# Score products of an attention kernel: the second head issued first, the first head's held behind it, in every item

## Chip, cores and metric

One core of a Trainium2 chip runs the whole program. The metric is the device time of one execution in microseconds (us). The kernel before took 1007.86 us, the median of 3 runs (1007.46 to 1009.16). About 0.2% (2.0 us) is what a measurement of this kernel can tell from no change.

## What is computed

Attention with a threshold, then two feed-forward layers, all in float32. Cut to what matters:

```python
# q, k, v: 4 batches, 8 heads, 576 positions, 64 per head
scores = (1 / sqrt(64)) * q @ k.T
thresh = max(scores, axis=-1) - tau
scores = where(scores >= thresh, scores, -1e9)
attn = exp(scores - max(scores));  attn /= sum(attn) + 1e-9
x = (attn @ v)            # as 2304 tokens x 512
h = x @ w_in              # 512 x 1024
solu = h * softmax(h);  ln = layernorm(solu) * g_ln
x2 = ln @ w_out           # 1024 x 512
y = softplus(x2 @ w2_in) @ w2_out   # 512 x 2048, 2048 x 512
```

## The kernel before, in words

Two heads make a pair: head 0 lies in partitions 0 to 63 of the tiles `q` and `k`, head 1 in partitions 64 to 127. The attention is cut into 36 items (`items`), each one pair of heads with one or two tiles of 128 query rows and, in some, a tail of 64 rows. Items 0 to 7 (`n < 2 * NPAIR`) have one tile each; the later ones have two, and 16 of those carry a tail (items 8 to 11, 16 to 19 and 24 to 31).

For each tile `scores` (L167 to L190) makes the 128 x 576 scores of both heads, each head in two matmuls of 288 columns (`nh` 0 and 1). Each is a float32 product, and in the trace it is two instructions of TensorE, so that a tile of both heads is eight instructions of L177. Head 0 goes to the PSUM tile `s0`, head 1 to `s1`; each has one buffer. A tail takes `s0` for both heads. VectorE then takes the row maximum of each head (`nm`, L187), ScalarE the exponential (`E`, L188), which frees the PSUM tile, and VectorE masks and sums (L195, in `mask`, up to one tile later).

Behind an item's scores come, for the item before it, the reciprocal of its sums (`rinv`, L238 and L239; `rb`, L245), the transposes of its exponentials (L210, L219, L221, L231, L250, copied out by ScalarE at L212, L224, L252), and for the item before that the product with `v` (L276, in `av`), which VectorE scales into `xr` (L279).

`m1_units` runs beside it: as soon as a unit of 256 tokens has all its heads, TensorE makes h (L355, twelve matmuls into one bank `w`), ScalarE copies it (L357), VectorE takes its maximum (`m_nm`, L367) and so on; L390 transposes, L403 makes `x2`. `prep_w1` splits the first layer's weights into two parts on VectorE (L81, L82, L84, L88, L118) and ScalarE (L80, L87); it fills the first 120 us. The second layer follows from about 500 us on (L573, L612).

The order in which the instructions stand on each engine is not the order of this code: a scheduler of the tile framework places them, by what it expects each tile's readiness to be. Engines take their instructions in that order, and wait by semaphores.

The flag `apart` decides the order of the four matmuls of a tile: head 0's two and then head 1's for items 0 to 7, the heads in turn (head 0 first) for the others. Nothing keeps the scheduler from placing something else between them.

Of the kernel before, what the change touches and what calls it, by code (L numbers as in the profile page):

```python
# [20 lines left out]
NPAIR = H // 2  # L21
# [12 lines left out]
def tile_attention_solu_softplus(ctx: ExitStack, tc: tile.TileContext, q, k, v, tau, w_in, w_out, g_ln, w2_in, w2_out, out):  # L34
    nc = tc.nc
    PSUM = bass.MemoryType.PSUM
    pe, dve, act, pool, sp = nc.tensor, nc.vector, nc.scalar, nc.gpsimd, nc.sync
# [107 lines left out]
    def qcol(h, i):  # L145
        return P * i if h == 0 else (64 + P * i if i < 4 else 0)
# [6 lines left out]
    def begin(n):  # L153
        it = Item()
        it.n = n
        it.b, h, it.ts, it.tail = items[n]
        it.p = it.b * NPAIR + h
        it.h = h
        it.nt = len(it.ts)
        it.W = P * it.nt  # L160
        it.E = []
        it.e = {}
        it.sums = at.tile([P, 5], F32, tag="sums", name=f"sums{n}", bufs=3)
        it.rinv = at.tile([P, 5], F32, tag="rinv", name=f"rinv{n}", bufs=3)
        return it

    def scores(it, k_, apart):  # L167
        z = st[it.p]
        tail = k_ == it.nt
        i = 4 if tail else it.ts[k_]  # L170
        ps = [psS.tile([P, 2, 512], F32, tag=f"s{h}", name=f"s{it.n}_{k_}_{h}") for h in range(1 if tail else 2)]
        order = [(nh, h) for h in range(2) for nh in range(2)] if apart else [(nh, h) for nh in range(2) for h in range(2)]
        for nh, h in order:
            r, c, m = slice(64 * h, 64 * h + 64), qcol(h, i), 64 if tail else P
            kc = (64 if h == 1 and tail else 0) + 288 * nh
            o = ps[0][r, nh, 0:288] if tail else ps[h][:, nh, 0:288]
            pe.matmul(o, z["q"][r, c:c + m], z["k"][r, kc:kc + 288], start=True, stop=True)  # L177
        if tail:
            it.T = at.tile([P, 640], F32, tag="T", name=f"T{it.n}")
        else:  # L180
            it.E.append(at.tile([P, 1152], F32, tag="E", name=f"E{it.n}_{k_}", bufs=4))
        for h in range(len(ps)):
            s = 2 * k_ + h
            E = it.T[:, 0:576] if tail else it.E[k_][:, 576 * h:576 * h + 576]
            sv = ps[h][:, :, 0:288]
            nm = at.tile([P, 1], F32, tag="nm", name=f"nm{it.n}_{s}", bufs=4)
            dve.tensor_reduce(out=nm, in_=sv, axis=AX.XY, op=ALU.max, negate=True)  # L187
            act.activation(out=E.rearrange("p (a b) -> p a b", a=2), in_=sv, func=AF.Exp, bias=nm, scale=1.0)  # L188
            pend.append((E, it.sums[:, s:s + 1]))
        return len(ps)  # L190

    def mask(keep):
        while len(pend) > keep:
            E, acc = pend.pop(0)
            dve.scalar_tensor_tensor(out=E, in0=E, scalar=etau, in1=E, op0=ALU.is_ge, op1=ALU.mult, accum_out=acc)  # L195
# [99 lines left out]
    def attention():  # L295
        cur = prev = pp = None
        for n in range(NI + 2):
            pp, prev, cur = prev, cur, (begin(n) if n < NI else None)
            work = []
            if prev is not None:  # L300
                per = 4 // prev.nt
                work.append(lambda: rinv(prev))
                if not prev.tail:
                    work.append(lambda: xrest(prev))
                for c0 in range(0, 8, per):
                    work.append(lambda c0=c0: xgroup(prev, c0))
                if prev.tail:
                    work += [lambda: xrest(prev), lambda: xtail(prev)]
                work.append(lambda: rgroup(prev))
            nk = cur.nt + cur.tail if cur is not None else 0  # L310
            slots = max(2 * nk, 1)
            for s in range(slots):
                if s % 2 == 0:
                    keep = scores(cur, s // 2, n < 2 * NPAIR) if cur is not None else 0
                    mask(keep)
                if s == 0 and pp is not None:
                    av(pp)
                    if last_use[pp.p] == pp.n and pp.b + 1 < B:
                        load_v(pp.p + NPAIR)

                a = len(work) * max(s - 1, 0) // max(slots - 1, 1) if slots > 1 else 0
                e_ = len(work) * s // (slots - 1) if slots > 1 else len(work)
                if s or slots == 1:
                    for w in work[a:e_]:
                        w()
                if s == slots - 1 and cur is not None:
                    m = n + 1
                    if m < NI and items[m][0] > 0 and (m == 0 or items[m - NPAIR][0] != items[m][0]):
                        scale_q(items[m][0] * NPAIR + items[m][1])
                yield  # L330
            if cur is not None and last_use[cur.p] == cur.n and cur.b + 1 < B:
                load_qk(cur.p + NPAIR)
# [291 lines left out]
    for i in range(len(seq) + LA):  # L624
        if i < len(seq):
            bi, c = seq[i]
# [64 lines left out]
```

## Time and profile before

| | us |
|---|---|
| median of 3 runs | 1007.86 |
| the profiled execution | 1010.33 |
| its span, first to last instruction | 1008.5 |
| TensorE (PE) busy | 948.4 (94%) |
| weight loads (PEld) busy | 747.2 (74%) |
| VectorE (DVE) busy | 713.4 (71%) |
| ScalarE (ACT) busy | 568.9 (56%) |
| mean granted TensorE clock | 0.971 of full speed |

A busy matmul is not TensorE at its peak: matmuls are pipelined, so that one row's time holds the tail of its pipeline, and the time from one start to the next tells what a run of them takes. Rows with an x and a number are several instructions in a row; in brackets stands the idle time of the engine before them and what ended it.

### The profile page before, as it was taken

To read this page: it belongs to the slowest core of one execution; us is meant where nothing else is said; L and a number is where in the kernel's file an instruction comes from. 1 tells how busy PE (TensorE), PEld (TensorE's weight loads), DVE (VectorE), ACT (ScalarE), POOL (GpSimd) and SP (SyncE) were. 2 spreads that over 40 slices of the span, in tenths; PEclk is the share of its full clock that TensorE was granted. 3 is DMA by queue.
4 is the path that set the end of the run, shared out by engine and by line. 5 is a ranking of instruction groups with operands and counts; after the bars stand their busy time and mean duration, and the time that the engine had idled before them with its cause. 6 is when DMAs were issued, how large, how long until landed. Compare 5 with 4: busy or idle time off the path is not lost.

```text
span 1008.5 us, 14610 instructions
## 1 busy us (share of the span) xinstructions
PE 948.4 (94%) x5664; PEld 747.2 (74%) x5664; DVE 713.4 (71%) x1387; ACT 568.9 (56%) x1082; POOL 75.1 (7%) x47
## 2 busy tenths in 40 slices
PE   3898999999999999999997699898999999999997
PEld 2666567777677777876886588676888788888896
DVE  5898866766768577676589959976555755665565
ACT  4765666666657567566556546544444444444453
POOL 0000000000000000000033534311001000000000
PEclk8898899999999999999998799998999999999999
DMA  8412200112001220000054533302000100100010
GB/s 220 173 61 79 75 27 12 35 44 78 27 11 36 65 69 15 12 11 6 33 162 141 162 127 103 125 1 84 1 0 22 63 1 1 42 1 0 1 44 21
DMA packets 27125, 55.21 MB, mean 55 GB/s; under 512 B 3248, under 2 KB 12464, under 8 KB 27056
## 3 DMA queue, kind: packets, MB, share of 16 engines
q1 hardware_dynamic: 26896, 53.99, 17.1%
q8 instruction: 44, 0.72, 0.3%
q10 hardware_dynamic: 160, 0.30, 0.1%
q14 instruction: 25, 0.20, 0.1%
HBM read 44.83 MB, written 9.44 MB: 54 GB/s over the span
## 4 chain that ended last, share of the span: by engine, by line
PE 67%; DVE 18%; ACT 8%; issue 3%; DMA 2%; SPq 0%; DVEq 0%; ACTq 0%
PE y L612 12%; PE h L573 12%; PE s L177 10%; PE w L355 9%; PE w L403 8%; PE w L276 7%; PE w L210 5%; DVE u L82 2%; DVE w L584 2%; DVE t L585 2%; DVE w L591 2%; DMA raw<-in_w_in_dram 2%; DVE u L84 2%; DVE w L592 1%; DVE gl L594 1%
## 5 line engine op out<-in xcount | busy, mean ns | idle before, releaser
L177 PE MATMUL s<-k,q 64*128 64x288 f32 (+1 forms) x640 | 135.0, 445 | 16.8 <-ACT q L143 8.9
L187 DVE TENSOR_REDUCE nm<-s 128x1 f32<-128x576 f32 x144 | 104.5, 750 | 43.4 <-PE s L177 43.4
L573 PE MATMUL h<-x2h,w2h 128*128 128x512 f32 (+1 forms) x320 | 119.3, 375 | 8.6 <-ACT x2h L541 7.0
L188 ACT ACTIVATE E<-s,nm 128x576 f32<-128x576 f32 x128 | 92.5, 741 | 52.6 <-DVE nm L187 52.4
L612 PE MATMUL y<-wo2h,gh 128*128 128x512 f32 x288 | 114.6, 398 | 7.5 <-ACT gh L593 4.3
L573 PE MATMUL h<-x2l,w2h 128*128 128x512 f32 (+1 forms) x320 | 118.8, 371 | 0.8 <-POOL x2l L542 0.8
L573 PE MATMUL h<-x2h,w2l 128*128 128x512 f32 (+1 forms) x320 | 118.6, 371 | 0.0
L612 PE MATMUL y<-wo2h,gl 128*128 128x512 f32 x288 | 113.8, 397 | 4.6 <-DVE gl L594 4.6
L612 PE MATMUL y<-wo2l,gh 128*128 128x512 f32 x288 | 113.4, 394 | 0.0
L195 DVE SCALAR_TENSOR_TENSOR E<-E,etau 128x576 f32<-128x576 f32 x128 | 102.5, 813 | 13.0 <-ACT E L188 9.1
L177 PEld LDWEIGHTS s<-k,q 64*128 64x128 f32 (+1 forms) x640 | 71.1, 182 | 53.8 <-issue 13.1
L586 ACT ACTIVATE w<-w 128x512 f32<-128x512 f32 (+1 forms) x80 | 47.1, 589 | 96.5 <-DVE t L585 96.4
L593 ACT CAST gh<-w 128x512 fp32r<-128x512 f32 (+1 forms) x80 | 46.2, 577 | 84.6 <-DVE w L592 84.3
L212 ACT COPY eT<-w 128x512 f32<-128x512 f32 x128 | 72.0, 592 | 24.2 <-PE w L210 23.7
L403 PE MATMUL w<-lh,wo1h 128*128 128x256 f32 x288 | 83.6, 291 | 0.0
L276 PE MATMUL w<-eT,v 128*64 128x256 f32 (+2 forms) x784 | 83.1, 357 | 0.0
L591 DVE SCALAR_TENSOR_TENSOR w<-h,w 128x512 f32<-128x512 f32 (+1 forms) x80 | 50.9, 637 | 44.7 <-ACT w L586 44.7
L403 PE MATMUL w<-ll,wo1h 128*128 128x256 f32 x288 | 81.5, 283 | 0.0
L403 PE MATMUL w<-lh,wo1l 128*128 128x256 f32 x288 | 81.4, 283 | 0.0
L594 DVE TENSOR_TENSOR gl<-w,gh 128x512 fp32r<-128x512 f32 (+1 forms) x80 | 51.0, 638 | 42.2 <-ACT gh L593 41.5
L276 PEld LDWEIGHTS w<-eT,v 128*64 128x64 f32 x784 | 52.8, 140 | 32.9 <-issue 9.7
L573 PEld LDWEIGHTS h<-x2h,w2h 128*128 128x128 f32 x320 | 61.4, 192 | 20.3 <-ACT x2h L541 7.2
(100 smaller groups left out, 1870.1 us busy)
## 6 DMA issues: line engine op xcount, KB each, us to landing
raw<-in_w_in_dram SPq DMA_DIRECT2D x16, 512.0 KB, 3.5
raw<-in_w_out_dram SPq DMA_DIRECT2D x16, 512.0 KB, 3.5
v<-in_v_dram SPq DMA_DIRECT2D x16, 320.0 KB, 3.0
x2s<-x SPq DMA_DIRECT2D x36, 128.0 KB, 1.7
x2r<-x2s SPq DMA_DIRECT2D x9, 512.0 KB, 4.0
q<-in_q_dram SPq DMA_DIRECT2D x30, 144.0 KB, 3.0
raw<-in_w_in_dram SPq DMA_DIRECT2D x4, 1024.0 KB, 8.9
raw<-in_w_out_dram SPq DMA_DIRECT2D x4, 1024.0 KB, 5.0
```

Of the source, the lines that this page charges most:

```text
L177: pe.matmul(o, z["q"][r, c:c + m], z["k"][r, kc:kc + 288], start=True, stop=True)
L187: dve.tensor_reduce(out=nm, in_=sv, axis=AX.XY, op=ALU.max, negate=True)
L188: act.activation(out=E.rearrange("p (a b) -> p a b", a=2), in_=sv, func=AF.Exp, bias=nm, scale=1.0)
L195: dve.scalar_tensor_tensor(out=E, in0=E, scalar=etau, in1=E, op0=ALU.is_ge, op1=ALU.mult, accum_out=acc)
L212: act.copy(out=eT, in_=bk)
L276: pe.matmul(o[64 * h:64 * h + 64, :], w_, e, start=(i == 0), stop=(i == 4))
L355: pe.matmul(ps, x_[:, c, P * t:P * t + P], w_[:, c, 512 * n:512 * n + 512], start=(j == 0), stop=(j == 11))
L403: pe.matmul(o, w_[:, c, P * m:P * m + P], l_[:, c, :], start=(j == 0), stop=(j == 23))
L573: pe.matmul(ps, w_[:, kc, :], x_[:, kc, 0:n], start=(j == 0), stop=(j == 11))
L591: dve.scalar_tensor_tensor(out=w_, in0=ps, scalar=0.0, in1=w_, op0=ALU.max, op1=ALU.add)
L594: dve.tensor_tensor(out=gl, in0=w_, in1=f(gh), op=ALU.subtract)
L612: pe.matmul(y, g_[:, P * j:P * j + P], w_, start=(c == 0 and i == 0), stop=(c == NC2 - 1 and i == 2))
```

## The change

`scores` loses the flag. In every item the order is now head 1, head 0, head 1, head 0, and head 0's first matmul carries an order-only dependency on head 1's first (without a semaphore), so that the scheduler may not place it ahead. A tail has the new order too, and no such dependency, since both its heads go to one PSUM tile.

```diff
-    def scores(it, k_, apart):
+    def scores(it, k_):
         z = st[it.p]
         tail = k_ == it.nt
         i = 4 if tail else it.ts[k_]
         ps = [psS.tile([P, 2, 512], F32, tag=f"s{h}", name=f"s{it.n}_{k_}_{h}") for h in range(1 if tail else 2)]
-        order = [(nh, h) for h in range(2) for nh in range(2)] if apart else [(nh, h) for nh in range(2) for h in range(2)]
-        for nh, h in order:
+        first = None
+        for nh, h in ((0, 1), (0, 0), (1, 1), (1, 0)):
             r, c, m = slice(64 * h, 64 * h + 64), qcol(h, i), 64 if tail else P
             kc = (64 if h == 1 and tail else 0) + 288 * nh
             o = ps[0][r, nh, 0:288] if tail else ps[h][:, nh, 0:288]
-            pe.matmul(o, z["q"][r, c:c + m], z["k"][r, kc:kc + 288], start=True, stop=True)
+            mm = pe.matmul(o, z["q"][r, c:c + m], z["k"][r, kc:kc + 288], start=True, stop=True)
+            if first is None:
+                first = mm
+            elif h == 0 and nh == 0 and not tail:
+                tc.add_manual_dep(mm.ins, first.ins.name, mybir.DependencyInfo(mybir.DependencyClass.NoSync, mybir.DependencyReason.DATA), reason="both heads side by side")
@@
-                    keep = scores(cur, s // 2, n < 2 * NPAIR) if cur is not None else 0
+                    keep = scores(cur, s // 2) if cur is not None else 0
```

The scheduler then places much else anew. Four lines more stand ahead of what follows, so a line of the text behind L177 has a number higher by four in the changed kernel (L276 is L280 there). In the rows below s6_0_1 is the score tile of item 6, its tile 0, head 1; w and a number is one bank of PSUM.

On TensorE, at item 6 in the first 60 us. Before:

```order
L210 MATMUL w23_442<-ident_98,E4_0_342 128x128 x4
L250 MATMUL w24_449<-ident_98,rb4_429 128x128
L355 MATMUL w25_461<-w1h_87,xh0_456 128x512
L355 MATMUL w25_461<-w1l_88,xh0_456 128x512
L355 MATMUL w25_461<-w1h_87,xl0_457 128x512
...
L276 MATMUL w26_492<-eT4_8_432,v0_123 64x128 x2
L276 MATMUL w26_492<-eT4_0_436,v0_123 64x128
L276 MATMUL w26_492<-eT4_4_443,v0_123 64x128
```

With the change:

```order
L214 MATMUL w23_442<-ident_98,E4_0_342 128x128 x4
L177 MATMUL s6_0_1_478<-k2_118,q2_117 128x288
L177 MATMUL s6_0_0_477<-k2_118,q2_117 128x288
L177 MATMUL s6_0_1_478<-k2_118,q2_117 128x288
L254 MATMUL w24_449<-ident_98,rb4_429 128x128
L177 MATMUL s6_0_0_477<-k2_118,q2_117 128x288
L359 MATMUL w25_461<-w1h_87,xh0_456 128x512
L359 MATMUL w25_461<-w1l_88,xh0_456 128x512
L280 MATMUL w26_492<-eT4_8_432,v0_123 64x128 x2
...
L359 MATMUL w25_461<-w1h_87,xl0_457 128x512
L280 MATMUL w26_492<-eT4_4_443,v0_123 64x128
```

The scores of item 6 stood ahead of the transposes (w21 to w23) and now stand behind them. Item 4's product with v (w26, ten matmuls) stood behind all twelve matmuls of h (w25); now nine of its matmuls stand behind the first two of w25, and the tenth still behind all twelve.

On VectorE, at the same place. Before:

```order
L81 TENSOR_SCALAR raw1_4_392<-raw1_4_392 128x1024
L279 TENSOR_TENSOR xr0_236<-w26_492,x4_451 128x128
L238 TENSOR_SCALAR rinv5_399<-sums5_398 128x2
L82 SCALAR_TENSOR_TENSOR w1_4_532<-w1_4_532,raw1_4_392 128x1024
L239 RECIPROCAL rinv5_399<-rinv5_399 128x2
L195 SCALAR_TENSOR_TENSOR E6_0_483,sums6_475<-E6_0_483,etau_105 128x576
L187 TENSOR_REDUCE nm7_0_584<-s7_0_0_577 128x1
L195 SCALAR_TENSOR_TENSOR E6_0_483,sums6_475<-E6_0_483,etau_105 128x576
L84 SCALAR_TENSOR_TENSOR w1_4_532<-raw1_4_392,w1_4_532 128x1024
```

With the change:

```order
L242 TENSOR_SCALAR rinv5_399<-sums5_398 128x2
L82 SCALAR_TENSOR_TENSOR w1_4_532<-w1_4_532,raw1_4_392 128x1024
L283 TENSOR_TENSOR xr0_236<-w26_492,x4_451 128x128
L243 RECIPROCAL rinv5_399<-rinv5_399 128x2
L199 SCALAR_TENSOR_TENSOR E6_0_483,sums6_475<-E6_0_483,etau_105 128x576 x2
L84 SCALAR_TENSOR_TENSOR w1_4_532<-raw1_4_392,w1_4_532 128x1024
L242 TENSOR_SCALAR rinv6_476<-sums6_475 128x2
L81 TENSOR_SCALAR raw1_5_530<-raw1_5_530 128x1024
L243 RECIPROCAL rinv6_476<-rinv6_476 128x2
L118 TENSOR_SCALAR w1_4_532<-w1_4_532,g_sb_137 128x512 x2
L371 TENSOR_REDUCE m_nm_550<-h0_0_460 128x1
```

The scaling of w26 into xr0 now has a step of the weights ahead of it, and the maxima of item 7 (nm7), which stood between the masks of item 6, now stand behind the maximum of h (m_nm).

On TensorE, at items 17 and 18, near 200 us. Before:

```order
L177 MATMUL s17_2_0_2035<-k5_902,q5_901 64x288
L210 MATMUL w124_2028<-ident_98,E16_0_1765 128x128
...
L177 MATMUL s17_2_0_2035<-k5_902,q5_901 64x288 x3
...
L403 MATMUL w130_2110<-lh1_1998,wo1l_90 128x256
L177 MATMUL s18_0_0_2146<-k6_1038,q6_1037 128x288
L177 MATMUL s18_0_1_2147<-k6_1038,q6_1037 128x288
```

With the change:

```order
L177 MATMUL s17_2_0_2035<-k5_902,q5_901 64x288 x2
L394 MATMUL w123_2021<-ident_98,h1_1_1618 128x128 x4
L177 MATMUL s17_2_0_2035<-k5_902,q5_901 64x288 x2
L177 MATMUL s18_0_1_2147<-k6_1038,q6_1037 128x288
L214 MATMUL w124_2028<-ident_98,E16_0_1765 128x128
...
L177 MATMUL s18_0_1_2147<-k6_1038,q6_1037 128x288
...
L177 MATMUL s18_0_0_2146<-k6_1038,q6_1037 128x288 x2
L280 MATMUL w131_2160<-eT16_8_2054,v4_948 64x256 x2
```

The four matmuls of item 18's first tile stood in a row, the heads in turn; now head 1's two stand singly near the tail of item 17, and head 0's two alone, some fifty instructions later. Items 25 and 26 read the same.

## Rows read from the trace of the kernel before

**Rows 1.** The page: granted clock in 40 slices, and the chain by engine.
```profile
PEclk8898899999999999999998799998999999999999
...
PE 67%; DVE 18%; ACT 8%; issue 3%; DMA 2%; SPq 0%; DVEq 0%; ACTq 0%
```
**Rows 2.** Busy time of each engine by stage: stretch, its length, engines, clock, DMA.
```profile
8.20:122.00 113.80, 95.16 (x593) 65.26 (x592) 99.50 (x206) 75.26 (x138) 0.00 (x0) 0.89 0.39 119
122.00:500.00 378.00, 375.76 (x2779) 285.70 (x2780) 262.32 (x614) 237.91 (x480) 0.00 (x0) 0.99 0.11 32
500.00:600.00 100.00, 83.13 (x512) 73.41 (x508) 76.23 (x126) 55.62 (x108) 38.53 (x22) 0.91 0.47 149
```
**Rows 3.** Timeline, scores of items 4, 6 and 8: start us, us, engine, line.
```profile
33.90 1.25 PE L177 MATMUL s<-k,q 64*128 64x288 f32 x8
...
42.22 1.23 PE L177 MATMUL s<-k,q 64*128 64x288 f32 x4 [0.86 <-ACT E L188]
...
44.42 1.24 PE L177 MATMUL s<-k,q 64*128 64x288 f32 x4 [0.97 <-ACT E L188]
...
63.04 1.24 PE L177 MATMUL s<-k,q 64*128 64x288 f32 x8
```
**Rows 4.** Waits of VectorE and TensorE, 5 to 135 us: total, times, longest.
```profile
DVE nm L187 <- PE s L177: 14.3, 9, 8.2
...
PE s L177 <- ACT E L188: 5.6, 6, 1.6
```
**Rows 5.** Timeline, VectorE's longer gaps in the first 100 us, and one product with v.
```profile
12.67 0.76 DVE L187 TENSOR_REDUCE nm<-s 128x1 f32<-128x576 f32 x1 [0.89 <-PE s L177]
...
14.27 0.70 DVE L81 TENSOR_SCALAR raw<-raw 128x1024 uint32<-128x1024 uint32 x1 [0.84 <-DMA raw<-in_w_in_dram]
...
30.93 0.76 DVE L187 TENSOR_REDUCE nm<-s 128x1 f32<-128x576 f32 x1 [1.43 <-PE s L177]
...
53.41 1.31 PE L276 MATMUL w<-eT,v 128*64 128x128 f32 x20
...
54.84 0.29 DVE L279 TENSOR_TENSOR xr<-w,x 128x128 f32<-128x128 f32 x1 [2.03 <-PE w L276]
...
92.35 1.22 DVE L367 TENSOR_REDUCE m_nm<-h 128x1 f32<-128x1024 f32 x1 [3.27 <-ACT h L357]
```
**Rows 6.** Group of the page: the exponential, count, busy us, mean ns of one.
```profile
L188 ACT ACTIVATE E<-s,nm 128x576 f32<-128x576 f32 x128 | 92.5, 741 | 52.6 <-DVE nm L187 52.4
```
**Rows 7.** Timeline, TensorE only: the tail of item 17 in two pieces, item 28's second tile.
```profile
203.97 0.69 PE L177 MATMUL s<-k,q 64*64 64x288 f32 x2
204.59 0.66 PE L210 MATMUL w<-ident,E 128*128 128x128 f32 x4
205.18 1.18 PE L177 MATMUL s<-k,q 64*64 64x288 f32 x6
206.29 0.66 PE L210 MATMUL w<-ident,E 128*128 128x128 f32 x4
...
375.08 1.96 PE L177 MATMUL s<-k,q 64*128 64x288 f32 x8
376.97 1.53 PE L210 MATMUL w<-ident,E 128*128 128x128 f32 x12
```
**Rows 8.** Timeline, TensorE only: item 35's first tile, in two pieces.
```profile
473.93 1.38 PE L177 MATMUL s<-k,q 64*128 64x288 f32 x4 [0.47 <-ACT E L188]
475.24 0.44 PE L250 MATMUL w<-ident,rb 128*128 128x128 f32 x2
...
478.64 0.76 PE L177 MATMUL s<-k,q 64*128 64x288 f32 x4
479.33 1.95 PE L276 MATMUL w<-eT,v 128*64 128x256 f32 x16
```
**Rows 9.** Two stretches at the lower clock: columns as in rows 2.
```profile
79.80:86.70 6.90, 6.90 (x21) 4.38 (x20) 6.90 (x16) 3.74 (x7) 0.00 (x0) 0.51 0.43 152
120.80:127.60 6.80, 6.80 (x23) 3.88 (x22) 3.95 (x10) 2.55 (x5) 0.00 (x0) 0.50 0.32 89
```

## The prediction

> **What bounds the kernel now.** I read the page first: its chain by engine is 67% TensorE and 18% VectorE, and the row of granted clock has its dips in the first 126 us, between 529 and 580, and once near 690 [rows 1]. Next the busy times by stage [rows 2]. They show three stages. From 8.2 to 122 us VectorE works 99.5 of 113.8 us (87%) at one attention item after another and at the weights; TensorE is counted 95.2 us busy there, at a mean clock of 0.89, but that counts the pipeline tails of short products. From 122 to 500 us TensorE is busy 375.8 of 378 us: there it alone sets the time. From 500 to 600 us no engine is full (the second layer's weights), and then TensorE again; no score product stands there, so whatever the change gains or loses ahead of 500 us is passed on.
>
> So two questions decide: does VectorE get through its 99.5 us sooner, and does TensorE have fewer cycles to spend between 122 and 500 us. VectorE's idle time in the front is small: it waited 14.3 us for scores in all, of which 8.2 is the start of the program [rows 4], and of its longer gaps three stand out: 1.43 us ahead of a maximum, 2.03 ahead of a scaling of the product with v, 3.27 ahead of the maximum of h [rows 5].
>
> **What the new order of the heads does by itself: next to nothing.** Item 4 was written one head after the other, and its eight instructions took 1.25 us; item 8, written in turn, took 1.24 [rows 3]. Item 6 was written like item 4 and took twice as long, four instructions in 1.23 us and, after 0.97 us of idle time, four in 1.24, because its second head waited for ScalarE's exponential to free s1 [rows 3]. So two heads run side by side in either order where both PSUM tiles are free, and apart only where the second is not.
>
> The Trainium skill, "TensorE: Matmul & The Clock Gate", Part 3, has it otherwise: matmuls start and end strictly in program order. By that rule item 4 would have run apart and each of the eight first items would now gain some 1.2 us of TensorE. Item 4's row speaks against it; the sum goes by the row, and the rule gets a small rival below.
>
> **What the pin does.** Head 0 now waits for s1 as well. Where TensorE waited for s1 anyway (item 6), head 1 ends as before, and so does TensorE; head 0 ends later by at least one exponential, 0.74 us [rows 6], and its maximum with it. I count nine such tiles in the front (items 1, 3, 5, 6, 7 and the second tiles of items 8 to 11): at most 9 x 0.74 = 6.7 us of delay, nothing if VectorE always has something else to do. VectorE is 87% busy there, so I let the uncovered 13% count: **+0.8 us**. Cover: the steps of the weights, which the new order puts into those places; without them the whole 6.7 would be due.
>
> **What the new order of the rest does, in the front.** Four places.
> - Item 1: the step L81 of the first weights, which waited for its DMA at 14.27 us, now stands ahead of item 1's first maximum, which ran at 12.67 [rows 5]. VectorE then idles through, and does that 0.76 us later: +0.8. Against it, the maximum of item 3 now has its scores early enough, since VectorE comes to it later and item 2's scores come sooner; half of the gap of 1.43 us [rows 5] should go: -0.7. Together **0**.
> - Item 6: the gap of 2.03 us. With the change a step L82 (1.2 us) stands ahead of the scaling and fills it. But w26 is complete only behind all of w25, since its tenth matmul stands there, and w25 now has most of w26's 1.31 us [rows 5] between its own. So the scaling starts some 0.4 us later than at 54.84, with 1.2 us of work done ahead of it: **-0.8**. Bounds: -2.0 (gap gone) to +0.4.
> - The gap of 3.27 us ahead of the second maximum of h at 92.35: it ends when 24 products of h have run, and part of them ran at the lower clock, 0.51 between 79.8 and 86.7 us [rows 9]. In the new order one more weight step L81 (0.70, the duration of the row at 14.27 [rows 5]) stands ahead of that maximum, and item 9's second tile runs as pairs for the most part, some 0.5 us shorter. **-1.2**; bounds 0 (the gap moves) and -3.3.
> - Everything else there: as before, by the same number of instructions with the same work.
>
> Front: 0.8 + 0 - 0.8 - 1.2 = -1.2 us.
>
> **Between 122 and 500 us**, where each TensorE cycle counts. A tile side by side takes 1.24 us, about 1.2 to the next start. Items 18 and 26: their first tile is torn into head 1, head 1 and twice head 0. A lone matmul of one head costs 0.62 (203.97 to 204.59 [rows 7]), head 0's two 1.23 [rows 3]: 2.47 in place of 1.2, so +1.3 each, **+2.6**. The tails of items 17 and 25 took 0.62 + 1.11 (205.18 to 206.29) [rows 7] and now run as two pairs of 0.62: -0.5 each, **-1.0**. Item 28's second tile took 1.89 to the next start [rows 7] and now stands later, whole: **-0.7**. Item 35's first tile took 1.31 + 0.69 [rows 8] and is whole now: **-0.8**. Items 17 and 25, second tile: three matmuls in a row and one behind the twelve of h, with the same count of lone ones as before: 0. Bounds: if the torn tiles hide beside neighbours, -2.5; if the joined ones save nothing, +2.6. Sum: +0.1. The maxima that come later by this have cover, as TensorE is the late one there.
>
> **Sum:** -1.2 + 0.1 = -1.1 us. The profiled execution took 1010.33 us, 2.5 above the median, so the sum gives 1009.2 for an execution like it and **1006.8 us** against the median of 1007.86.
>
> **Rivals.**
> - *A dip of the clock gone.* At 120.8 to 127.6 us TensorE ran at half clock, 1.2 GHz, just as it became the bound [rows 9], behind two waits for exponentials; VectorE was busy only 3.95 of those 6.8 us. If the new order spares that dip, 3.4 us of TensorE's work comes back: 1006.8 - 3.4 = 1003.4 us. For it: the dip follows idle time, which the new order shifts. Against: item 11's tail and item 12 still wait for exponentials there.
> - *A further dip, slower.* TensorE has less to do while it waits for s1, and it already idled 5.6 us for exponentials in the front [rows 4]. If one more stretch of 6.8 us at half clock falls where VectorE waits for products (as at 79.8 to 86.7), it costs up to 3.4 us and the front's gain with it: 1007.9 + 0.1 + 3.4 = 1011.4 us. It decides once the pin's waits leave TensorE idle longer than the 0.86 to 0.97 us of item 6 [rows 3] in several tiles running. For it: the mean clock of 0.89 in the front shows how near the edge it is. Against: the work that now stands ahead of the pinned products keeps it busy. The Trainium skill, on the same page, Part 1, has the throttled clock as the default, which activity lifts; the rows agree.
> - *Strict order.* By the rule of Part 3 the eight first items gain on TensorE; VectorE's waits for scores bound it, 14.3 - 8.2 = 6.1 us [rows 4]: 1001.8 us.
> - *No effect*, the scheduler's shifts cancel: 1007.9 us.
>
> **How the numbers follow.** Forecast 0.47 (own range 1004.5 to 1008.8: the sum and about half of its bounds on either side), a dip gone 0.20, a further dip 0.25, strict order 0.04, no effect 0.04. Of the forecast 0.15 lies beyond 0.2% (2.0 us, what a measurement can tell) on the fast side, 0.30 within, 0.02 on the slow side. Faster: 0.15 + 0.20 + 0.04 = 0.39; same: 0.30 + 0.04 = 0.34; slower: 0.02 + 0.25 = 0.27. The range reaches to the two dips: 1002.4 to 1011.4 us.
>
> **What would show it.** In the changed kernel's timeline all score tiles of items 0 to 7 as eight instructions in about 1.24 us (longer only at half clock); VectorE's gap near 55 us at about 1 us, the one near 92 us at about 2; the time from item 13's scores to the end of the attention as long as before; the torn tiles of items 18 and 26 as rows of x2, x2 and x4. Wrong, if VectorE's idle time between 8 and 122 us grows, if the count of half-clock stretches ahead of 150 us changes, or if the front ends as before and the time between 122 and 500 us moves by over 2 us.

## The result: 1021.2 us, slower by 1.25%, outside the range

| | before | with the change |
|---|---|---|
| median (runs) | 1007.82 (4) | 1021.21 (4) |
| lowest to highest | 1007.46 to 1009.16 | 1017.99 to 1023.98 |
| the profiled execution | 1010.33 | 1022.65 |
| its span | 1008.5 | 1020.9 |
| mean granted clock | 0.971 | 0.971 |

The ratio is 1.0125, with a 95% interval of 1.0105 to 1.0145. Forecast were 1006.8 us, in a range of 1002.4 to 1011.4.

The page of the changed kernel, first the row of the granted clock and then the chain that ended last, by engine [rows 1]:

```profile
PEclk8899899999999999999998799999999999999999
...
PE 63%; DVE 20%; ACT 10%; issue 3%; DMA 3%; ACTq 0%; DVEq 0%; SPq 0%
```

TensorE's share of the chain fell from 67 to 63%, VectorE's and ScalarE's rose. The busy times of the same stages [rows 2] (us; then busy time and count of TensorE, its weight loads, VectorE, ScalarE and GpSimd, the granted clock, the DMA share, GB/s):

```profile
8.20:122.00 113.80, 91.27 (x603) 62.10 (x599) 101.97 (x211) 76.88 (x142) 0.00 (x0) 0.91 0.37 119
122.00:500.00 378.00, 372.74 (x2715) 279.80 (x2713) 256.60 (x597) 231.00 (x465) 0.00 (x0) 0.99 0.11 31
500.00:600.00 100.00, 84.28 (x543) 75.05 (x542) 76.35 (x131) 55.97 (x114) 36.56 (x21) 0.91 0.45 144
```

Between 122 and 500 us TensorE now works 372.7 us in place of 375.8: where it alone sets the time, it stood still for 3 us more (the two stretches don't hold quite the same work; from item 14 to item 35's second tile its idle time is 4.5 us in place of 2.2). The loss came in three parts. Item 14's first scores start at 149.11 us (before 146.81: **+2.3**), item 35's second tile at 491.77 (before 484.88: +6.9, so **+4.6** between them), and the execution took 12.3 us longer, so **+5.4** lie in code that the change doesn't touch.

Three words are used from here on. The *front* is all that stands ahead of item 14's first scores; the *pin* is the order-only dependency that holds one head's first product behind the other's; a tile is *torn* when its products don't run in one piece.

The front. VectorE's gaps there [rows 5] are these now:

```profile
55.43 0.29 DVE L283 TENSOR_TENSOR xr<-w,x 128x128 f32<-128x128 f32 x1 [4.35 <-PE w L280]
...
92.14 1.23 DVE L373 SCALAR_TENSOR_TENSOR u<-h,u 128x1024 f32<-128x1024 f32 x1 [0.50 <-ACT u L372]
...
121.59 0.82 DVE L199 SCALAR_TENSOR_TENSOR T<-T,etau 128x576 f32<-128x576 f32 x1 [1.35 <-ACT T L192]
...
126.76 1.42 DVE L191 TENSOR_REDUCE nm<-s 128x1 f32<-128x576 f32 x2 [3.91 <-PE s L177]
...
131.43 0.42 DVE L283 TENSOR_TENSOR xr<-w,x 128x256 f32<-128x256 f32 x1 [2.28 <-PE w L280]
```

The gap of 3.27 us ahead of the second maximum of h is gone (that maximum starts at 89.02, without a wait), and 0.50 is left ahead of the step behind it; the gap at 55 us is 4.35 in place of 2.03, and the two near 126 and 131 us are 3.91 and 2.28. The same two steps before:

```profile
128.37 1.42 DVE L187 TENSOR_REDUCE nm<-s 128x1 f32<-128x576 f32 x2 [2.41 <-PE s L177]
...
130.39 0.42 DVE L279 TENSOR_TENSOR xr<-w,x 128x256 f32<-128x256 f32 x1 [0.60 <-PE w L276]
```

So up to 122 us VectorE was ahead (idle for 11.8 of the 113.8 us, before 14.3), and it fell behind from there to item 14 (12.3 us idle, before 8.9). With the change TensorE sat idle ahead of these two gaps, as its timeline has it:

```profile
101.73 1.19 PE L177 MATMUL s<-k,q 64*64 64x288 f32 x8 [1.56 <-ACT E L192]
103.86 0.33 PE L225 MATMUL w<-ident,T 128*128 128x128 f32 x1 [0.95 <-DVE T L247]
...
117.22 0.33 PE L225 MATMUL w<-ident,T 128*128 128x128 f32 x1 [2.44 <-DVE T L247]
```

Then it ran at half clock, 1.2 GHz, for 13.6 us on end (before 6.8 [rows 9]; columns as above):

```profile
118.30:131.90 13.60, 13.60 (x61) 7.71 (x58) 5.82 (x16) 4.29 (x8) 0.00 (x0) 0.50 0.16 45
```

Items 17 and 18 on TensorE (items 25 and 26 are the same, row for row), first before and then with the change:

```profile
191.96 1.97 PE L177 MATMUL s<-k,q 64*128 64x288 f32 x8
...
196.27 1.90 PE L177 MATMUL s<-k,q 64*128 64x288 f32 x8
...
213.50 1.24 PE L177 MATMUL s<-k,q 64*128 64x288 f32 x8
...
220.52 1.24 PE L177 MATMUL s<-k,q 64*128 64x288 f32 x8
```

```profile
194.26 1.97 PE L177 MATMUL s<-k,q 64*128 64x288 f32 x8
...
199.24 1.23 PE L177 MATMUL s<-k,q 64*128 64x288 f32 x6 [0.70 <-ACT E L192]
...
203.64 0.75 PE L177 MATMUL s<-k,q 64*128 64x288 f32 x2
...
210.33 0.75 PE L177 MATMUL s<-k,q 64*128 64x288 f32 x2
...
217.77 1.23 PE L177 MATMUL s<-k,q 64*128 64x288 f32 x4
...
224.78 1.24 PE L177 MATMUL s<-k,q 64*128 64x288 f32 x8
```

The second tile of item 17 waits 0.70 us for s1 and is torn (x6, and x2 at 203.64); the first tile of item 18 is torn too (x2 at 210.33 and x4 at 217.77; its other two lie in the x6 row of the tail at 207.99). From 194.26 to 224.78 are 30.5 us; before it was 28.6.

### The profile page after: what moved, and what is told of

The parts are those of the page before. It is cut to its first block, busy times and chain, and to the rows that moved or that the text cites. A ratio compares the mean times of both kernels' runs of the same rounds, so it can differ in the third digit from the quotient of the medians.

```text
span 1020.9 us, 14639 instructions
## 1 busy us (share of the span) xinstructions
PE 949.2 (93%) x5664; PEld 745.3 (73%) x5664; DVE 714.0 (70%) x1387; ACT 567.0 (56%) x1082; POOL 74.9 (7%) x47
## 4 chain that ended last, share of the span: by engine, by line
PE 63%; DVE 20%; ACT 10%; issue 3%; DMA 3%; ACTq 0%; DVEq 0%; SPq 0%
PE h L577 12%; PE y L616 11%; PE s L177 10%; PE w L359 9%; PE w L407 8%; PE w L280 7%; PE w L214 4%; DVE u L82 2%; ACT E L192 2%; DVE w L588 2%; DVE t L589 2%; DVE w L595 2%; DVE w L596 2%; DMA out_dram<-yo 2%; DVE u L84 1%
## 5 line engine op out<-in xcount | busy, mean ns | idle before, releaser
L177 PE MATMUL s<-k,q 64*128 64x288 f32 (+1 forms) x640 | 130.4, 449 | 23.8 <-ACT E L192 12.7
L177 PEld LDWEIGHTS s<-k,q 64*128 64x128 f32 (+1 forms) x640 | 67.6, 183 | 60.3 <-ACT E L192 19.5
L192 ACT ACTIVATE E<-s,nm 128x576 f32<-128x576 f32 x128 | 90.1, 740 | 34.0 <-DVE nm L191 33.9
L199 DVE SCALAR_TENSOR_TENSOR E<-E,etau 128x576 f32<-128x576 f32 x128 | 101.1, 813 | 10.2 <-ACT E L192 7.5
L280 PE MATMUL w<-eT,v 128*64 128x256 f32 (+2 forms) x784 | 88.4, 364 | 0.3 <-ACT eT L216 0.3
L280 PEld LDWEIGHTS w<-eT,v 128*64 128x64 f32 x784 | 55.3, 143 | 36.5 <-issue 14.0
```

The lines of the kernel that those rows point to most:

```text
L177: mm = pe.matmul(o, z["q"][r, c:c + m], z["k"][r, kc:kc + 288], start=True, stop=True)
L280: pe.matmul(o[64 * h:64 * h + 64, :], w_, e, start=(i == 0), stop=(i == 4))
```

## The experiments

There were fifteen runs, of thirteen further kernels and of the two kernels once more, each with the kernel before beside it (its median was 1008.2 to 1008.6). The intervals are those of the ratio to it.

| kernel | median us (lowest to highest) | ratio, 95% interval |
|---|---|---|
| pin_to_7 | 1014.73 (1009.88 to 1018.17) | 1.0059, 1.0037 to 1.0081 |
| pin_from_8 | 1019.27 (1016.97 to 1023.75) | 1.0108, 1.0089 to 1.0127 |
| order_no_pin | 1010.51 (1003.16 to 1014.61) | 1.0012, 0.9994 to 1.0030 |
| h0_first_pinned | 1002.33 (999.26 to 1004.55) | 0.9937, 0.9921 to 0.9954 |
| no_pin_17_25 | 1018.51 (1016.46 to 1018.73) | 1.0089, 1.0074 to 1.0104 |
| no_pin_8_12 | 1022.17 (1017.43 to 1025.49) | 1.0125, 1.0104 to 1.0146 |
| after_again, before_again | 1020.44, 1007.72 (one run each) | |
| before_plus_24 | 1013.80 (1012.05 to 1016.92) | 1.0055, 1.0036 to 1.0074 |
| after_plus_60 | 1015.27 (1011.88 to 1017.58) | 1.0058, 1.0038 to 1.0078 |
| h0_pin_from_8 | 1003.92 (1003.66 to 1004.45) | 0.9956, 0.9940 to 0.9971 |
| turns_no_pin | 1007.70 (1006.34 to 1011.89) | 0.9995, 0.9982 to 1.0008 |
| after_h0_8_13 | 1018.01 (1011.68 to 1020.85) | 1.0081, 1.0054 to 1.0108 |
| undo_two | 1011.19 (1006.45 to 1016.75) | 1.0029, 1.0011 to 1.0047 |
| undo_three | 1010.16 (1004.61 to 1012.48) | 1.0011, 0.9997 to 1.0025 |

### Order or pin, early items or late

Four kernels take the change apart. pin_to_7 has it for items 0 to 7 alone, pin_from_8 for items 8 to 35 alone; order_no_pin keeps the order and drops the pin; h0_first_pinned turns both round.

```diff
 pin_to_7 (pin_from_8: the other way round, with before's order for items 0 to 7)
-        for nh, h in ((0, 1), (0, 0), (1, 1), (1, 0)):
+        for nh, h in (((0, 1), (0, 0), (1, 1), (1, 0)) if it.n < 8 else ((0, 0), (0, 1), (1, 0), (1, 1))):
-            elif h == 0 and nh == 0 and not tail:
+            elif h == 0 and nh == 0 and not tail and it.n < 8:
 order_no_pin
-            elif h == 0 and nh == 0 and not tail:
+            elif False:
 h0_first_pinned
-        for nh, h in ((0, 1), (0, 0), (1, 1), (1, 0)):
+        for nh, h in ((0, 0), (0, 1), (1, 0), (1, 1)):
-            elif h == 0 and nh == 0 and not tail:
+            elif h == 1 and nh == 0 and not tail:
```

> Items 0 to 7 as in the changed kernel (head 1 first, head 0 pinned), items 8 to 35 as before (heads in turn from head 0, no pin). On TensorE the order then differs from before in the front alone. Theory A (each stage pays for itself: front +2.3 us at item 14's scores, attention after it +4.6, second layer +5): the front's +2.3 stays and 122 to 500 us is as before: 1007.8 + 2.3 = 1010 us, and 1015 if the second layer loses 5 by whatever comes late into it. Theory B (the long half-clock stretch at 118 to 132 us is made by the pinned tiles of items 8 to 12 just there): the stretch is short again, about 7 us, and the time 1007 to 1009. Theory C (the scheduler's other placement of the weights' steps in the first 60 us is the whole cause): 1018 to 1021.

> Items 0 to 7 as before (one head after the other, no pin), items 8 to 35 as in the changed kernel. TensorE's order is the changed kernel's from about item 10 on. Theory A: the stretch from 122 to 500 us loses its 4.6 us again (waits for s1, torn first tiles of items 18 and 26): 1007.8 + 4.6 = 1012.4 us, and 1017 if the second layer loses its 5 with it. Theory B: 4.6 and the front's 2.3 as well: 1014.7, or 1020 with the second layer's. Theory C: within 2 us of before.

> The changed kernel without the order-only dependency: head 1, head 0, head 1, head 0 for every item, but the scheduler may put head 0's products ahead of the first of head 1. If the pin is the cause (head 0 and all behind it wait for s1): 1007 to 1010 us, the waits for ScalarE's exponential ahead of item 17's and 25's second tile gone, the torn tiles gone. If the order of the heads or the new placement is the cause: 1018 to 1021 us.

> A pin the other way round: head 0, head 1, head 0, head 1 for every item, head 1's first product pinned behind head 0's first. Its place differs from before in 134 of TensorE's 4824 instructions (the changed kernel: 273). If waiting for s1, the tile that comes free last, is what the pin costs, this one waits only for s0 and the time is 1006 to 1009 us. If any pin tears tiles and holds back TensorE: 1012 us or more.

From item 14 to item 35 the traces repeat each other to 0.1 us, so that stage can be read from one profile each. Against before it gains or loses: pin_from_8 +4.7 (item 14 at +0.43, item 35's second tile at +5.10), the changed kernel +4.6, pin_to_7 +0.1, order_no_pin -0.7, h0_first_pinned +0.4. So there it is the pin behind head 1 in the late items, and neither the order nor a pin as such: a pin of head 1 behind head 0 costs at most 0.4 us there, as s0 comes free first. The time as a whole agrees for order_no_pin (1010.5, at the edge of the pin theory's 1007 to 1010). h0_first_pinned is below its 1006 to 1009 and **faster than both kernels**, by 0.6% than before. pin_to_7 came out above its 1010: its front lost 4.8 us, with 37.5 us of half clock ahead of 150 us (before 30.7), and 2.2 us were lost behind item 35. So its 1014.7 is theory A's 1015 in number, but not in its parts. pin_from_8 lost more than its 4.7 as well: 8.3 us behind item 35. Its 1019.3 is near theory B's 1020, but not in B's way, since its front lost 0.4 us. No theory so far told where these losses come from.

### The two pins of items 17 and 25

```diff
 no_pin_17_25
-            elif h == 0 and nh == 0 and not tail:
+            elif h == 0 and nh == 0 and not tail and not (it.n in (17, 25) and k_ == 1):
```

> The changed kernel without the pin on the second tile of items 17 and 25 alone; TensorE's order then differs from the changed kernel's in 28 of 4824 instructions, and the first tiles of items 18 and 26 stand whole again. If those two pins cause both the wait for s1 and the torn tile behind it: from item 17's first tile to item 18's second takes as long as before (28.6 us; changed kernel 30.5), the same at items 25 and 26, so that 122 to 500 us loses some 0.7 to 0.9 us in place of 4.6, and the time is 1021.2 - 3.9 = 1017.3 us. If the pairs and tears cost nothing and something else slows that stage: 30.5 us again, 1021.

```profile
193.55 1.97 PE L177 MATMUL s<-k,q 64*128 64x288 f32 x8
...
197.86 1.90 PE L177 MATMUL s<-k,q 64*128 64x288 f32 x8
...
215.08 1.24 PE L177 MATMUL s<-k,q 64*128 64x288 f32 x8
...
222.09 1.24 PE L177 MATMUL s<-k,q 64*128 64x288 f32 x8
```

TensorE's timeline of that kernel has both tiles whole again, and 28.5 us from 193.55 to 222.09, the same at items 25 and 26. Item 14 to item 33 loses 0.9 us in place of 4.8. So these two pins are 3.9 us of the stage; the medians say 2.7 (1021.21 to 1018.51). What stays is 0.5 at items 21 and 22 and 0.7 at item 28, less 0.3 that come back by item 33.

### Is the rest of the kernel or of the execution?

The changed kernel and the kernel before ran once more for a second profile each, and no_pin_8_12 leaves the pin out in the items of the long half-clock stretch.

```diff
 no_pin_8_12
-            elif h == 0 and nh == 0 and not tail:
+            elif h == 0 and nh == 0 and not tail and not 8 <= it.n <= 12:
```

> The changed kernel once more, for a second profile of it. If its places of half-clock and the waits at the bounds of the second layer's blocks belong to the kernel: the same stretches (43 to 54, 118 to 132, 801 to 805 us), item 14's scores at +2.3 us against before, the last stage +4.6 again. If they belong to the execution: other places, and only the +4.6 us between items 14 and 35 is the same.

> The kernel before once more, for a second profile. If the stretches at half clock belong to the kernel: 18 to 29, 45 to 53, 79 to 87, 120 to 128, 697 to 705 us again, all rows within 0.3 us of the first profile. If they belong to the execution: other places; the stage from item 14 to item 35 takes the same 338.1 us within 0.3.

> The changed kernel without the pin in items 8 to 12. If the pinned tiles there make TensorE idle and with that the long half-clock stretch at 118 to 132 us: that stretch is 7 us long, item 14's scores come within 1 us of before (now +2.3), the time is 1018 us. If the dips of the front fall by the phase of VectorE's and TensorE's work and not by the pin: the sum of half-clock time ahead of 150 us is as it falls (20 to 38 us were seen in five kernels), item 14's scores anywhere from -3 to +5 us, and that sum predicts where.

The long stretch of the changed kernel came again, 13.7 us from 116.3 on, with item 14 at +1.85, and so did waits in the second layer. In before_again the stretch of 10.2 us near 18 us was gone, and every later row up to the end of the attention stood 2.65 us earlier: such stretches in the front come and go with the execution. For no_pin_8_12 the result lies between the theories: no half clock at 118 to 132 us, as the first had it, but 20.5 us of it between 66 and 94, and no gain in time.

The front can be judged from this table, with VectorE's idle time ahead of 100 us and from there to item 14 (us, from the trace's rows; "half clock" is the time at 1.2 GHz):

| kernel | VectorE idle, 8 to 100 | VectorE idle, 100 to item 14 | TensorE idle there | half clock there | half clock ahead of 150 | item 14 against before |
|---|---|---|---|---|---|---|
| before | 12.5 | 9.8 | 2.0 | 6.8 | 30.7 | 0 |
| before_again | 10.7 | 9.2 | 2.0 | 6.8 | 20.5 | -2.7 |
| before_plus_24 (same front) | 14.7 | 6.7 | 2.0 | 0 | 37.5 | -1.1 |
| changed kernel | 9.7 | 14.7 | 6.3 | 13.7 | 30.7 | +2.3 |
| after_again | 9.6 | 14.2 | 6.3 | 13.7 | 27.3 | +1.9 |
| undo_two (same front) | 10.0 | 13.1 | 6.3 | 10.2 | 20.5 | +1.1 |
| pin_from_8 | 11.9 | 10.7 | 5.4 | 6.8 | 23.9 | +0.4 |
| pin_to_7 | 17.0 | 9.5 | 3.0 | 6.8 | 37.5 | +4.8 |
| no_pin_8_12 | 18.7 | 5.9 | 3.6 | 0 | 37.5 | +2.6 |
| after_h0_8_13 | 15.2 | 6.4 | 4.4 | 3.4 | 27.3 | +0.1 |
| undo_three (same front) | 10.6 | 5.0 | 4.3 | 0 | 10.2 | -6.6 |
| h0_first_pinned | 8.8 | 5.4 | 2.0 | 3.4 | 23.9 | -8.2 |

From 8 to 100 us kernels with the same front differ by 4 us and more, with long half-clock stretches between 62 and 95 us where the idle time is long. From 100 us to item 14 VectorE's idle time goes by the half-clock time there: 5.0 to 6.7 us with 0 to 3.4 us of it, 9.2 to 10.7 with 6.8, 13.1 to 14.7 with 10.2 to 13.7. TensorE's idle time there goes by the kernel: 5.4 to 6.3 us with head 0 pinned behind head 1 in items 8 to 13, 2.0 to 4.4 without. That the pin makes TensorE idle there is shown by this. That it brings the long half-clock stretch is likely (10.2 us or more came with this pin alone), but not shown, since pin_from_8 has the pin and 6.8 us. The front as a whole does lose: five profiles with the changed kernel's front have item 14 at +1.1 to +2.3 us, three with before's at -2.7 to 0, which is 2.9 us between the means. Which of its pins cost that isn't settled: those of items 0 to 7 alone lost 4.8 us in the one profile of pin_to_7, and without those of items 8 to 12 no_pin_8_12 stood at +2.6.

### The second layer: a packet of instructions

What the second layer waits for stands in the view of the output DMA, as who waited for it (us, times). Before, the changed kernel, and two kernels with more products in front of the second layer:

```profile
  ACT yo L616: 1.4, 2
```

```profile
  ACT yo L620: 6.2, 4
  DVE yo L620: 3.0, 3
```

At the end of each block four banks are copied out through two buffers, so that the third and the fourth copy wait for the output DMAs of the first two. Before, and then with the change, where these DMAs came late:

```profile
699.90 0.58 ACT L616 COPY yo<-y 128x512 f32<-128x512 f32 x1 [0.70 <-DMA out_dram<-yo]
```

```profile
700.58 0.80 PE L612 MATMUL y<-wo2h,gh 128*128 128x512 f32 x1 [1.07 <-DVE yo L616]
```

```profile
709.63 0.59 ACT L620 COPY yo<-y 128x512 f32<-128x512 f32 x1 [1.79 <-DMA out_dram<-yo]
```

```profile
709.74 0.50 PE L616 MATMUL y<-wo2h,gh 128*128 128x512 f32 x1 [2.33 <-DVE yo L620]
```

The block's fourth copy, on ScalarE, waited 1.79 us for the DMA in place of 0.70, and TensorE, behind the copies, 2.33 us in place of 1.07. The DMA queues around the first two output DMAs of this block, 4 us before and 4.5 us with the change (packets, MB, share of 16 engines, and under them the DMAs with their median time to landing), show why:

```profile
q1 hardware_dynamic: 601, 0.78, 53.9%
...
out_dram<-yo SPq DMA_DIRECT2D x2, 256.0 KB, 2.0
```

```profile
q1 hardware_dynamic: 522, 0.74, 45.2%
q8 instruction: 1, 0.02, 1.6%
...
out_dram<-yo SPq DMA_DIRECT2D x2, 256.0 KB, 3.3
```

One packet of 16 KB, the next piece of an engine's program, falls among the output's packets, and takes 1.13 us on its DMA engine; the output lands after 3.3 us in place of 2.0. Before, it came at 701.61, when these two had landed. There it fell on the third and the fourth output DMA of the block (699.5 to 702.5 us):

```profile
q8 instruction: 1, 0.02, 3.4%
...
out_dram<-yo SPq DMA_DIRECT2D x2, 256.0 KB, 4.3
```

They landed later still, but no copy of the block waits for these two. In all 17 profiles each output DMA that took over 3 us (73 of 340) met such a packet, which started from 0.1 us ahead of its issue to 2.2 us behind it; those that met none took 2.0 to 2.8. Such packets come every 29 us here, which is 128 weight loads and 128 products at 0.227 us a pair: it is TensorE's program, 256 instructions a time. The Trainium skill, "Runtime: NRT & Kernel Launch", section on the mechanics of instruction fetch, has the same 16 KiB and 256 instructions; it calls their cost mostly hidden. For TensorE the trace agrees (from 720 to 780 us, across two packets, its products start 0.225 to 0.228 us apart), but not for the DMAs beside them.

The change shifts them, because it gives TensorE more instructions to fetch: the waits that stand alone ahead of the score products (x is their number; before, with the change, and in order_no_pin).

```profile
L177 PEldq EVENT_SEMAPHORE  x45: 51/51/899, 4.4 to 418.1; - x45
```

```profile
L177 PEldq EVENT_SEMAPHORE  x73: 51/51/450, 6.1 to 489.5; - x73
```

```profile
L177 PEldq EVENT_SEMAPHORE  x66: 51/51/51, 5.7 to 478.5; - x66
```

In all, 79 such instructions of TensorE stand ahead of the first output before, 103 with the change (counted in the trace). The order alone, without the pin, has 97. To try it, before got 24 more instructions and the changed kernel 60, as idle products whose results are overwritten:

```diff
 before_plus_24 (after_plus_60: range(30))
+        if (bi, c) == (0, 0):
+            for _ in range(12):
+                pe.matmul(ps[:, 0:64], w2h[0][:, 0, :], w2h[0][:, 0, 0:64], start=True, stop=True)
```

> The kernel before with twelve further products of 64 columns into the first bank of the second layer, overwritten by what follows: 24 more instructions (weight load and product) in TensorE's stream, mostly in its idle 7 us at 563 to 570 us. The changed kernel has 24 more instructions in that stream than before by the first output (103 wait instructions in place of 79). In its trace a 16 KB packet of the instruction queue comes 1.1 us behind the first output DMA of a block, in before 4.9 us behind; in the first case the copies into the output's two buffers wait 9.2 us in all for output DMAs, in the second 1.4. If the place of that packet makes the second layer's loss: here it comes 1 to 2.5 us behind, the waits are 5 us or more, and the time is 1010 to 1014 us. If the loss comes with the attention's own change or its lateness: 1.4 us of waits and 1008 to 1009.

> The changed kernel with thirty such products: 60 more instructions in TensorE's stream, so that the packet should come 5 us ahead of each block's first output DMA. If its place makes the second layer's loss: waits for output DMAs back at 1.4 us, the time from the first L577 product to the end as before, and 1021 - 4 = 1017 us, less a us for the products that don't fit into the idle time. If not: 1021 to 1022.

```profile
  ACT yo L619: 5.8, 4
  DVE yo L619: 0.8, 1
```

```profile
  ACT yo L623: 1.4, 2
```

Both came as the packet theory had them: 6.6 us of waits made in the one, 1.4 left in the other, and the medians moved by +5.4 (1008.44 to 1013.80) and -5.9 (1021.21 to 1015.27). In the profiled executions the last stage itself moved by +4.1 and by -2.4 to -3.1. Where the rest of the medians' change lies isn't shown; fronts that differ from run to run are the likely place. The last stage, from the 25th product of the second layer's first line to the end of the span, sorts all profiles by the place of the packet:

| kernel | packet behind the first output DMA of blocks 1 to 3, us | last stage, us |
|---|---|---|
| before, before_again, h0_first_pinned, h0_pin_from_8 | 4.8 to 6.5 | 415.2 to 415.3 |
| turns_no_pin | 5.0 to 5.9 | 413.0 |
| pin_to_7 | 4.9 to 6.5 | 417.2 |
| after_plus_60, undo_two, undo_three | -12.0 to -7.4 | 417.0 to 417.2 |
| before_plus_24, order_no_pin, after_h0_8_13 | 1.1 to 2.9 | 419.3 |
| changed kernel, after_again, no_pin_17_25 | 1.0 to 2.0 | 419.4 to 420.5 |
| no_pin_8_12, pin_from_8 | 1.1 to 2.1 | 423.2, 423.5 |

In nine profiles the packet misses the first two output DMAs of these blocks (in six of them it meets the last two): 413.0 to 417.2 us, and 1.4 us of waits for output DMAs in each. In eight it meets the first two: 419.3 to 423.5 us, and 5.8 to 12.7 us of waits. Not all of the spread is the packet's, for the half-clock time in this stage differs too: 3.4 us in turns_no_pin, 18.6 and 18.8 in no_pin_8_12 and pin_from_8, 7.7 to 14.3 in the others. The cleanest pair is the changed kernel and after_plus_60, with the same half-clock time in every block: there the packet costs 3.1 us. The other 1.8 us of the stage's 4.8 stay in after_plus_60; they lie in its first three blocks alone, whose half-clock time is 6.8, 0 and 3.4 us where before had 3.4, 6.8 and 0.

### The front again, and the sum

```diff
 h0_pin_from_8 (items 0 to 7 in before's order)
+        for nh, h in (((0, 0), (0, 1), (1, 0), (1, 1)) if it.n >= 8 else ((0, 0), (1, 0), (0, 1), (1, 1))):
+            elif h == 1 and nh == 0 and not tail and it.n >= 8:
 turns_no_pin
+        for nh, h in ((0, 0), (0, 1), (1, 0), (1, 1)):
+            elif False:
 after_h0_8_13 (elsewhere as in the changed kernel)
+        lead = 0 if 8 <= it.n < 14 else 1
+        for nh, h in (((0, 0), (0, 1), (1, 0), (1, 1)) if lead == 0 else ((0, 1), (0, 0), (1, 1), (1, 0))):
+            elif h == 1 - lead and nh == 0 and not tail:
```

undo_two joins no_pin_17_25 and after_plus_60; undo_three joins after_h0_8_13 to them.

> Items 0 to 7 as before, the others head 0 first with head 1 pinned behind it. The pin of head 1 in every item gave 1002.3 us; from items 14 to 35 that kernel stood at a constant -8.2 to -7.8 us against before. If its gain is made by items 8 to 13 (item 12's first tile in one piece, no half clock at 116 to 130 us): 1002 to 1004 us. If by items 0 to 7: 1007 to 1009.

> Both heads in turn from head 0 for every item, no pin: TensorE's order differs from before in 12 of 4824 instructions, in items 0 to 7 alone. If each tile's own order is worth nothing and the front's time follows the larger placement: 1007 to 1010 us. If matmuls of one head behind the other cost their full time in the first items: 1002 us.

> The changed kernel, with head 0 first and head 1 pinned behind it in items 8 to 13 alone. If waiting for s1 in these items makes the loss between 100 us and item 14: VectorE's idle time there falls from 14.5 us to 6 to 10 and TensorE's from 6.3 to about 3, the half-clock stretch at 116 to 130 us shrinks, item 14's scores come 4 to 7 us sooner, and the time is 1014 to 1017 us. If the dips of the clock fall as they will, whatever the pin: no sooner than before by over 2 us, 1019 to 1022.

> The changed kernel without the pin on the second tiles of items 17 and 25, and with thirty products of 64 columns ahead of the second layer, whose results are overwritten. If these two parts add up: 1021.2 - 2.7 to 3.9 (items 17 and 25) - 5.9 (the packet) = 1011.4 to 1012.6 us, which leaves the front's 3 to 4 us to before. If they overlap: 1014 or more.

> All three undone: head 0 first and pinned the other way in items 8 to 13, no pin on the second tiles of items 17 and 25, thirty products ahead of the second layer. Head 1 still goes first, with head 0 behind it, in all other items. If the three parts are the whole loss: 1005 to 1009 us, no slower than before. If something else of the change costs time: 1011 or more.

h0_pin_from_8 keeps most of h0_first_pinned's gain, with items 0 to 7 as before, and from item 14 on it is no faster than before (338.0 us to item 35's second tile, before 338.1; the same last stage): the gain is made by items 8 to 13. There TensorE's timeline of h0_first_pinned has item 12's first tile in one piece, while before had it in two, 6.25 us apart (120.36 and 126.61 us), with a half-clock stretch in between [rows 9]:

```profile
118.10 1.31 PE L177 MATMUL s<-k,q 64*128 64x288 f32 x8
```

undo_two came 0.2 us below the sum's 1011.4 to 1012.6, at 1011.19: the two parts add up to 10.0 of 13.4 us. Its profile, 9.0 us shorter than the changed kernel's, gives back 3.9 us between item 14 and item 35 and 3.0 in the last stage; the rest is 1.2 in the front and 0.9 between. after_h0_8_13 missed its 1014 to 1017 by a us: VectorE's idle time behind 100 us fell to 6.4 as expected, but a half-clock stretch of 13.7 us at 65 us gave it back in the profiled run. undo_three missed too, at 1010.16 for 1005 to 1009, though its interval doesn't tell it from before; its profiled run (1006.8, with 10.2 us of half clock in the front) was among the faster of runs from 1004.6 to 1012.5. What the front's part is worth in the medians isn't clear of noise: the interval of after_h0_8_13 overlaps the changed kernel's, and undo_three's overlaps undo_two's. So TensorE's idle time in items 8 to 13 is shown to be the pin's, its price in time is not. What decides, execution by execution, where in the front the clock is halved stays open, and with it the front's 2 to 3 us.

## Why the prediction was wrong, by its steps

- **"Whatever the change gains or loses ahead of 500 us is passed on."** The step that failed most: 5.4 of the 12.3 us between the two profiles come behind item 35, 4.8 of them in the last stage (415.2 to 420.1). TensorE's 24 further instructions bring the packet in among each block's first output DMAs, which is 3.1 us of it; the other 1.8 go with where that stage has the clock halved. No step of the prediction counted instructions other than the products.
- **"Items 17 and 25, second tile ... 0."** These two pins are 3.9 us. I had seen three products in a row and a lone one, and not asked what the pinned product waits for: s1, freed 0.70 us late, and behind the wait the scheduler tears this tile and the next. The torn tiles of items 18 and 26 were right as rows (x2, x2, x4), and their +2.6 near (3.9 less two waits of 0.70 is 2.5), but as effects of that pin.
- **Items 28 and 35, -0.7 and -0.8.** Item 28's tile ran whole and the stage still lost 0.7 there; item 35 gave back 0.3. Items 21 and 22 cost 0.5 that stood nowhere.
- **The front, -1.2.** The prediction's front ends at 122 us, and up to there it gained: VectorE's idle time fell from 14.3 to 11.8 us. The loss stands behind 122 us, where the prediction had no term for the front. **The pin's +0.8** was mis-sized with it, and its cover misjudged: VectorE's 87% is a mean, and the last step of the weights starts at 114.69 us. From 100 us to item 14 VectorE's idle time rose from 9.8 and 9.2 us to 14.7 and 14.2, beside more idle time of TensorE's own (6.3 us in place of 2.0) and twice the half-clock time there. How the loss divides between these two stays open.
- **The gap near 92 us, -1.2.** Right in kind and more than forecast (3.27 to none, and 0.50 behind). **The gap near 55 us, -0.8**: wrong as a gap, 4.35 us where about 1 was forecast, because VectorE came to it sooner (51.08 us in place of 52.81). But the scaling started 0.6 us later (54.84 to 55.43; forecast 0.4), with VectorE's idle time up to there 7.7 us in place of 8.5, so the price of -0.8 was near.
- **The new order by itself, nothing.** Right for the tiles: turns_no_pin is the same within 0.2%, and with the change the tiles of items 3, 4, 5 and 7 ran as eight instructions in 1.24 us. Item 6 did not, against the forecast: six instructions at half clock from 44.31 on, the last two behind a transpose at 46.93, 3.95 us in all. But the order has a price of its own that the forecast left out: order_no_pin has 18 more wait instructions than before and a last stage of 419.3 us; in its profile it gained 3.4 us in the front and 0.7 in the attention against that. The rule of the Trainium skill, "TensorE: Matmul & The Clock Gate", Part 3, of strict order in start and end, would have given it the gain of the rival on strict order, 1001.8 us; it didn't come.
- **The rival of a further dip** named TensorE's idle time as the cause: it was 0.95 to 2.44 us in several tiles running, ahead of 13.6 us at half clock. But no stretch was added: ahead of 150 us there are three in place of four, with the same sum of 30.7 us; one doubled and one went. That undo_two, without the two other parts, took its 1011.4 (1011.19) is chance. I gave it 0.25, and the range ended there, as no case held two losses at once.
- **The range's low end, 1002.4 us**, follows from nothing in the working; the rival that it is said to reach to has 1003.4.

## What to carry to other kernels

A pin that makes an early-ready product wait behind a late one is paid where the engine is the bound, and again where the scheduler fills the hole with pieces; pin the late one behind the early one, which made the whole kernel 0.6% faster here, all of it ahead of item 14. Count the wait instructions that an order adds to a stream, too: what lies hundreds of us later can shift against its DMAs, and a small edit can be judged by that shift rather than by itself. So look at the stages behind the change, and if they moved, shift them alone before the change is blamed for them.

## What was not expected of the hardware

- A packet of 16 KB of TensorE's program, 0.9 to 1.7 us long on one DMA engine, delayed a 256 KB output DMA from 2.0 us to 3.1 to 4.7. Through two buffers, at the ends of up to four blocks, this cost 3.1 us of the last stage where the half-clock time was the same (420.1 and 417.0).
- The granted clock of the same front differed between executions: 30.7 and 20.5 us at 1.2 GHz ahead of 150 us in before's two profiles, 37.5 in before_plus_24, with up to 4 us more of idle time on VectorE; behind 150 us the attention repeated to 0.1 us.
- Ahead of a long half-clock stretch TensorE had idled: 1.56, 0.95 and 2.44 us in the changed kernel ahead of 118 us.
